# The last stage of a linear-attention and soft-MoE kernel: second layer and outputs by 256, 128 and 128 columns in place of 256 and 256, and a new order of steps on TensorE

## The chip, the cores and the metric

The kernel runs on one core of a Trainium2 chip. The metric is the device time of one execution in microseconds (us), lower is better. The runs of the kernel before took 341.94, 344.8 and 346.77 us, so the median is 344.8 us. One more execution was profiled; all rows of the trace are from that one.

A core has TensorE (PE: matmuls, with the weight loads listed as PEld), VectorE (DVE), ScalarE (ACT), GpSimd (POOL) and SyncE (SP), whose queue issues all DMAs of this kernel.

## The reference

Eight batches of eight heads of 576 tokens go through a linear attention with exponential features, and its output, 4608 tokens of 512 columns, through a soft mixture of eight experts with four slots each:

```python
q_p, k_p = phi(q), phi(k)                      # exp(+-(x w_phi - max|.|)), 256 features
kv  = einsum('bhsf,bhsd->bhfd', k_p, v)
x   = (q_p @ kv) / (q_p @ sum_s k_p + 1e-6)    # 4608 x 512 once the heads are side by side

logits = x @ phi                               # 4608 x 32 (8 experts x 4 slots)
d = softmax of logits over the 4608 tokens
slot_input = d.T @ x                           # 32 x 512
for e in range(8):
    h = maximum(slot_input[e] @ w1[e], 0)      # w1[e]: 512 x 1024
    slot_out[e] = h @ w2[e]                    # w2[e]: 1024 x 512
c = softmax of logits over the 32 slots
out = c @ slot_out                             # 4608 x 512
```

Only the last two products, `h @ w2[e]` and `c @ slot_out`, are touched by the change. All expert slots must be known before a single token can be written, so the whole output, 9.44 MB, leaves the core at the end.

## The kernel before

**Up to the last stage.** A list of tasks (`Plan`, with `ORDER` as the order written out by hand) runs the attention, the logits and the dispatch sums for the first 284 us or so. Weights are loaded in between, each of the 64 weight tiles (128 x 1024, 512 KB) with one DMA on SP's queue (L235): 32 tiles of `w1`, then 16 tiles of `w2` for output columns 0 to 255, then 16 tiles for columns 256 to 511. The later tiles reuse space that the attention gives back, and so are loaded late.

**The last stage** begins at L963. TensorE's instructions are issued there in exactly the order in which the program writes them (`manual_schedule(engines={PE})`); instructions of the other engines are put in order by the framework's scheduler, and start when their data is there. SP's queue issues the output DMAs one after the other.

- `layer1` (L841) makes `hp`, `hidden` (L894, L895) applies the maximum and the scale, and `picked` (L903, L906) turns the result and puts it into `sh`, with zeros in the places of other experts' slots.
- `layer2(a, e, cs)` (L932, L935) is the second layer of one expert for the 256 columns of half `a`. It is a sum over eight chunks `c` of 128 hidden units. A matmul has 32 weight columns (the slots) and 256 moving columns (of `w2`); four chunks run side by side in four column groups of the array. Every matmul stands in the trace as two instructions, so an expert and a half take 16 rows.
- `slots(a)` (L941, DVE) copies the sum out of PSUM. `slots2(a, ys)` (L948, L951) adds the four groups with a matmul by `rep` into `psy`, and an ACT copy and a DVE operation after it split the result into a rounded value and its rest: `yr`.
- `repeated(i)` (L617, POOL) and `combine(i)` (L921, L925, L926) prepare `cT[i]`, the combine weights of token group `i` (512 tokens, nine groups): four transposes on TensorE into `psc`, a rounding copy on ACT, and a subtraction on DVE that puts the rest in the lower half. Groups 0 to 2 are prepared earlier (L626, L630, L636); groups 3 to 8 in this stage.
- `output(a, i, yr)` (L959, L960, L961) makes 256 columns of 512 tokens: two matmuls with 512 moving columns into two of four PSUM banks, one copy by DVE and one by ACT into a tile `o`, and one 512 KB DMA. The matmul reads `yr` and `cT[i]`. The copies have to free a bank before the second next output can use it.

The order is a string: `C` is `combine` of the next group, `L` half an expert of `layer2` for columns 256 to 511, `o` the next output of columns 0 to 255, `r` is `slots2` of the first half, `s` and `R` are `slots` and `slots2` of the second. The nine outputs of the second half follow behind the string:

```python
TAIL = "CCLLrLLoLLCoLLCoLLCoLLCoLLoLoLsoRo"
```

Of the kernel before, what the change touches and what calls it, by code (L numbers as in the profile page):

```python
# [9 lines left out]
F32 = mybir.dt.float32  # L10
F32R = mybir.dt.float32r
AF = mybir.ActivationFunctionType
ALU = mybir.AluOpType
# [16 lines left out]
DM, NE, SPE, FF = 512, 8, 4, 1024  # L30
NS = NE * SPE
KC = DM // 128
FC = FF // 128
SP, PE, ACT, DVE, POOL = (getattr(mybir.EngineType, n) for n in ("SP", "PE", "Activation", "DVE", "Pool"))
NTT = B * S // 128
DH = DM // 2
# [7 lines left out]
NCT = 3  # L44
# [73 lines left out]

TAIL = "CCLLrLLoLLCoLLCoLLCoLLCoLLoLoLsoRo"


@with_exitstack
def tile_kernel(ctx: ExitStack, tc, xT, vv, w, phi, w1, w2, cst, out):
# [7 lines left out]
    nc = tc.nc  # L134
# [46 lines left out]
    for i in range(NWARM):  # L181
        ps = pmm.tile([128, 512], F32, tag="mm", name="psw")
# [9 lines left out]
    cs = const.tile([128, 257], F32, name="cs")  # L192
    ident = cs[:, 0:128]
    rep = cs[:, 128:256]
    low4 = cs[:, 256:257]
# [23 lines left out]
    keep = [10, 11, 12, 13]  # L219
    order = [j for j in range(nslot[-1]) if j not in keep]  # L220
    wt = []
    wpools = [wpool]

    def slot(j, name, dt=F32):
        return wpools[sum(j >= n for n in nslot)].tile([128, 1024], dt, tag=f"w{j}", name=name)
# [387 lines left out]
    cT = []  # L613
# [41 lines left out]
    for b in range(NB + 2):  # L655
# [10 lines left out]
        for p, (b_, u, t0, t1) in enumerate(pieces):  # L666
            if b_ == b:
                new, end = t0 == 0 or p == 0 or pieces[p - 1][0] != b, 4 * b + 4 == NT * u + t1
                n = t1 - t0
# [6 lines left out]
        q, bank = b - 2, [f"qb{b % 2}"]  # L676
# [6 lines left out]
    for s in range(NK):  # L683
        u, c = divmod(s, NCH)
        bp, h = divmod(u, H)
        n = bp, c
# [6 lines left out]
        if end:  # L693
            d = pick("kvcopy") == "d"
            p = max(i for i in range(len(pieces)) if pieces[i][1] == u)
# [21 lines left out]
        n = last_of[c] if final else 2 * bp + c // 2  # L717
# [119 lines left out]
    def layer1(a, kcs):  # L837
        for kc in kcs:
            for n in range(2):
                for e in range(4):  # L840
                    nc.tensor.matmul(hp[a][32 * e:32 * e + 32, n], si[:, kc],  # L841
                                     wt[(a * KC + kc) * 4 + e][:, n * 512:(n + 1) * 512],
                                     start=kc == 0, stop=kc == KC - 1, skip_group_check=True)
# [26 lines left out]
    def bank(shape, name):  # L870
        cps.append(cps.pop(0))
        return cps[-1][0].tile(shape, F32, tag=cps[-1][1], name=name)

    def lastw():
        for c in range(NCH):
            n = last_of[c]
            ps = bank([128, G, NS], "psL")
            turned(lTs.pop(n), ps)
            l = sm.tile([128, G, NS], F32, tag="eT", name="ls", bufs=3)
            nc.vector.tensor_copy(l, ps)  # L880
            wmax(n, l)
            wsub(n, nc.vector)
            wexp(n)
            wsum(n)
            wdiv(n, nc.vector)

    sh = []
# [4 lines left out]
    def hidden(a):  # L892
        t = slot(keep[a], "hs")
        nc.scalar.activation(t[:, 0:512], hp[a][:, 0], AF.Relu, scale=rs)  # L894
        nc.vector.tensor_scalar(t[:, 512:1024], hp[a][:, 1], rs, 0.0, op0=ALU.mult, op1=ALU.max)  # L895
        return t

    def picked(a, t):
        for i in range(2):
            ps = bank([128, FC // 2, 4, NS], "psh")  # L900
            for c in range(FC // 2):
                o = (FC // 2 * i + c) * 128
                nc.tensor.transpose(ps[:, c].rearrange("p e s -> p (e s)"), t[:, o:o + 128], ident)  # L903
            for e in range(4):
                c0 = (4 * a + e) * SPE
                nc.vector.tensor_copy(sh[a][:, e, FC // 2 * i:FC // 2 * (i + 1), c0:c0 + SPE], ps[:, :, e, c0:c0 + SPE])  # L906


    spare = [order[i] for i in range(len(wsrc) - nslot[-1], len(order)) if order[i] < NE * KC]
    gone = [i if i < nslot[-1] else order[i - nslot[-1]] for i in range(NE * KC, NE * (KC + 2))]  # L910
    cws, cts = [], []

    def repeated(i):
        if i % 2:
            cws.append(slot(spare[6 + i // 2 - 1], "cw").rearrange("p (g m) -> p g m", g=2))
        four(cws[-1][:, 1 - i % 2].rearrange("p (j m) -> p j m", m=128), i)

    def combine(i):
        ps = pd.tile([128, 4, 128], F32, tag="c", name="psc")
        for j in range(4):  # L920
            nc.tensor.transpose(ps[:, j], cws[(i - NCT) // 2][:, 1 - i % 2, j * 128:(j + 1) * 128], ident)  # L921
        if i % 2:
            cts.append(slot(spare[i // 2 - 1], "cT", F32R).rearrange("p (g m) -> p g m", g=2))
        x, ps = cts[-1][:, 1 - i % 2], ps.rearrange("p j m -> p (j m)")
        nc.scalar.copy(x, ps)  # L925
        nc.vector.tensor_tensor(x[64:128], ps[64:128], x[64:128].bitcast(F32), op=ALU.subtract)  # L926
        cT.append(x)


    yp = ph[0].tile([128, 2, 512], F32, tag="h", name="yp")  # L930

    def layer2(a, e, cs=range(FC)):  # L932
        for c in cs:
            g = 32 * (c % 4)
            nc.tensor.matmul(yp[g:g + 32, a, 0:DH], sh[e // 4][:, e % 4, c],  # L935
                             wt[NE * KC + (a * NE + e) * 2 + c // 4][:, (c % 4) * DH:(c % 4 + 1) * DH],
                             start=(e == 0 and c < 4), stop=(e == NE - 1 and c >= 4), skip_group_check=True)

    def slots(a):
        ys = slot(spare[3 + a], "ys")[:, 0:DH]  # L940
        nc.vector.tensor_copy(ys, yp[:, a, 0:DH])  # L941
        return ys

    yrs = slot(spare[5], "yr", F32R)

    def slots2(a, ys):
        ps = pd.tile([128, DH], F32, tag="c", name="psy")
        nc.tensor.matmul(ps, rep, ys, start=True, stop=True)  # L948
        yr = yrs[:, DH * a:DH * a + DH]

        yis = [nc.scalar.copy(yr, ps), nc.vector.scalar_tensor_tensor(yr, yr.bitcast(F32), low4, ps, op0=ALU.mult, op1=ALU.add)]  # L951
        return yr, yis[0].ins, yis[-1].ins

    def output(a, i, yr):

        o = slot(gone[i] if a == 0 else (gone[9:16] + keep[0:2])[i], "o").rearrange("p (b t) -> p b t", b=2)
        for b in range(2):
            ps = bank([128, 512], "pso")
            nc.tensor.matmul(ps, yr[:, b * 128:(b + 1) * 128], cT[i], start=True, stop=True)  # L959
            (nc.scalar.copy if b else nc.vector.tensor_copy)(o[:, b], ps)  # L960
        nc.sync.dma_start(out[a, i], o.rearrange("p b t -> p (b t)"))  # L961

    NO = NTT // 4  # L963
    with tc.manual_schedule(engines={PE}):
        layer1(1, range(0, 1))
        lastw()
        layer1(1, range(1, 2))
        picked(0, hidden(0))
        layer1(1, range(2, KC))
        layer2(0, 0)  # L970
        layer2(0, 1)
        picked(1, hidden(1))
        stacks["h"].close()
        pd = ctx.enter_context(tc.tile_pool(name="pd", bufs=2, space=PSUM, reuse_waits="tile"))
        for i in range(NCT, NO):
            repeated(i)
        for e in range(2, NE):
            layer2(0, e)
        ys = slots(0)
        cs, outs, l2 = iter(range(NCT, NO)), iter(range(NO)), iter(range(2 * NE))  # L980
        behind = ExitStack()
        for step in TAIL:
            if step == "L":
                e, i = divmod(next(l2), 2)
                layer2(1, e, range(4 * i, 4 * i + 4))
            elif step == "C":
                combine(next(cs))
            elif step == "o":
                output(0, next(outs), yr)
            elif step == "s":  # L990
                ys = slots(1)
            elif step == "r":
                yr, *_ = slots2(0, ys)
            else:
                yr2, *ins = slots2(1, ys)
                for x in ins:
                    behind.enter_context(tc.issue_after(x))
        behind.close()
        for i in range(NO):
            output(1, i, yr2)  # L1000


# [34 lines left out]
```

## Time and profile before

| what | value |
|---|---|
| runs | 341.94, 344.8, 346.77 us; median 344.8 |
| profiled execution | 344.9 us, of which the span of the trace 343.1 us |
| mean granted TensorE clock in the span | 0.984 of full speed |
| output DMAs | 18 of 512 KB, first issued at 313.73 us |
| median time of an output DMA from issue to landing | 3.7 us |

Rows of the timeline read: start in us, duration in us, engine, line, operation, tile written <- tiles read, shape, count of merged instructions, and in brackets the idle time of the engine ahead of it with what ended it. Rows of the chain of waits have start, duration, engine, tile and line; the chain is followed back from the last instruction. Rows of windows have, for a stretch of the span, the busy time (and number of instructions) of each engine, the granted TensorE clock as a share of full speed, the busy share of the DMA engines and the GB/s that they moved. In the views of DMA the GB/s are given in 40 equal slices of the stretch asked for. Matmuls overlap, so the durations of rows of single matmuls add up to more than the time that passes.

### The profile page before, as it was taken

Reading aid. Unit: us, or ns where it says so; the run is one execution under the profiler, and the core shown is the slowest. Engines: PE = TensorE matmul, PEld = TensorE weight load, DVE = VectorE, ACT = ScalarE, POOL = GpSimd, SP = SyncE. Lnnn points to the kernel's source line nnn. Section 1 sums busy time; section 2 is a strip of 40 time slices with the busy share of each in tenths; the row PEclk is TensorE's granted clock in tenths of the full one; section 3 lists DMA queues with packets and bytes.
Section 4 is the critical chain, followed back from the end, with each engine's and each line's share of the span. In section 5 each row is a group of like instructions: output and inputs, shape, how many; then the busy total and the mean of one; then the engine's idle time right before and its main releaser. Section 6 shows DMA issues by size and latency. Waiting matters only on the chain.

```text
span 343.1 us, 16153 instructions
## 1 busy us (share of the span) xinstructions
PE 327.2 (95%) x6825; PEld 271.1 (79%) x6825; DVE 243.6 (71%) x683; ACT 233.2 (68%) x677; POOL 168.0 (49%) x353
## 2 busy tenths in 40 slices
PE   8997999999999999999999999999999999999970
PEld 4896899998979999998899998979998753355430
DVE  1576487987787888887888888688886562615780
ACT  3897489968867888777789978677886250204470
POOL 1546466872356867561758758256664511130000
PEclk9999899999999999999999999999999999999995
DMA  6377256267234654674262844495426979998698
GB/s 223 117 238 257 83 196 226 67 208 285 66 111 155 204 166 165 210 302 118 58 195 61 320 154 149 162 319 176 128 76 233 352 297 406 408 406 333 282 400 324
DMA packets 22649, 74.09 MB, mean 216 GB/s; under 512 B 2992, under 2 KB 3248, under 8 KB 22576
## 3 DMA queue, kind: packets, MB, share of 16 engines
q1 hardware_dynamic: 22576, 73.05, 60.1%
q8 instruction: 54, 0.88, 1.0%
q14 instruction: 19, 0.16, 0.1%
HBM read 63.60 MB, written 9.44 MB: 213 GB/s over the span
## 4 chain that ended last, share of the span: by engine, by line
PE 92%; DVE 2%; ACT 2%; issue 1%; POOL 1%; ACTq 0%; POOLq 0%
PE kvp L311 23%; PE psn L364 20%; PE psq L264 12%; PE psk L264 10%; PE psx L734 5%; PE yp L935 4%; PE hp L841 4%; PE pso L959 3%; PE psl L417 2%; PE pss L456 2%; PE psw L183 1%; PE psc L921 1%; PE psd L449 1%; PE pss L559 1%; PE psh L903 1%
## 5 line engine op out<-in xcount | busy, mean ns | idle before, releaser
L284 POOL TENSOR_TENSOR vs<-vt,mk 128x520 f32<-128x520 f32 (+3 forms) x128 | 91.6, 730 | 63.3 <-ACT mk L273 42.6
L311 PE MATMUL kvp<-vs,kf 128*64 128x65 f32 (+1 forms) x2304 | 93.3, 230 | 1.9 <-issue 1.9
L311 PEld LDWEIGHTS kvp<-vs,kf 128*64 128x64 f32 x2304 | 81.8, 138 | 9.3 <-issue 5.4
L364 PE MATMUL psn<-kvs,qf 128*64 128x65 f32 x2304 | 82.1, 222 | 0.8 <-issue 0.8
L264 PE MATMUL psq<-xs,wd 64*128 64x128 f32 x576 | 78.7, 284 | 0.0
L264 PE MATMUL psk<-wd,xs 64*128 64x128 f32 x576 | 77.4, 283 | 0.6 <-ACT kf L298 0.4
L364 PEld LDWEIGHTS psn<-kvs,qf 128*64 128x64 f32 x2304 | 74.5, 138 | 3.4 <-issue 1.4
L264 PEld LDWEIGHTS psq<-xs,wd 64*128 64x128 f32 x576 | 69.2, 190 | 3.7 <-issue 1.1
L264 PEld LDWEIGHTS psk<-wd,xs 64*128 64x128 f32 x576 | 68.4, 190 | 4.1 <-ACT kf L298 1.3
L269 DVE TENSOR_REDUCE mk<-psk 128x4 f32<-128x512 f32 x72 | 48.4, 678 | 17.2 <-PE psk L264 8.0
L331 ACT ACTIVATE qf<-psq 128x512 f32<-128x512 f32 x72 | 42.7, 595 | 20.0 <-DVE mts L326 5.9
L326 DVE TRANSPOSE_TENSOR_REDUCE mts<-psq 128x16 f32<-128x512 f32 x72 | 50.7, 706 | 7.6 <-PE psk L264 3.6
L295 ACT ACTIVATE kf<-psk 128x512 f32<-128x512 f32 x72 | 42.6, 592 | 18.7 <-DVE mk L269 7.6
L406 POOL TENSOR_TENSOR xc<-un,dn 128x256 f32<-128x256 f32 x64 | 39.2, 614 | 12.6 <-PE pss L456 6.6
L375 DVE TENSOR_TENSOR un<-psn,eq 128x195 f32<-128x195 f32 x96 | 33.1, 348 | 16.3 <-PE psn L364 12.6
L334 ACT ACTIVATE qf<-psq 128x512 f32<-128x512 f32 x72 | 42.9, 601 | 0.4 <-DVE mts L326 0.2
L298 ACT ACTIVATE kf<-psk 128x512 f32<-128x512 f32 x72 | 42.6, 596 | 0.0
L342 ACT ACTIVATE mh<-mts 32x36 f32<-32x36 f32 x128 | 29.4, 230 | 7.5 <-DVE mts L326 5.9
L380 DVE TENSOR_TENSOR un<-psn,un 128x195 f32<-128x195 f32 x96 | 33.2, 349 | 1.1
L348 DVE TENSOR_REDUCE eq<-mh 32x9 f32<-32x36 f32 x128 | 26.4, 206 | 2.6 <-ACT mh L342 1.1
L272 ACT ACTIVATE mk<-mk 128x4 f32<-128x4 f32 x72 | 15.1, 210 | 4.0 <-DVE mk L269 3.4
L351 POOL TENSOR_TENSOR eq<-eq 128x9 f32<-128x9 f32 x32 | 6.5, 203 | 22.0 <-DVE eq L348 22.0
(130 smaller groups left out, 342.4 us busy)
## 6 DMA issues: line engine op xcount, KB each, us to landing
wt<-w SPq DMA_DIRECT2D x64, 512.0 KB, 7.0
xs<-xT SPq DMA_DIRECT2D x36, 512.0 KB, 4.2
vt<-vv SPq DMA_DIRECT2D x32, 325.0 KB, 3.3
out<-o SPq DMA_DIRECT2D x18, 512.0 KB, 3.7
xs<-xT SPq DMA_DIRECT2D x2, 128.0 KB, 2.5
cs<-cst SPq DMA_DIRECT2D x1, 128.5 KB, 4.0
wd<-w SPq DMA_DIRECT2D x1, 64.0 KB, 2.1
phs<-phi SPq DMA_DIRECT2D x1, 64.0 KB, 3.8
```

The lines of the kernel that those rows point to most:

```text
L264: nc.tensor.matmul(ps, l, r, start=True, stop=True)
L269: nc.vector.tensor_reduce(km[b][:, 2], kx[b], axis=AX, op=ALU.max, apply_absolute_value=True)
L284: nc.gpsimd.tensor_tensor(vs[b][:, :, place(b, u, t, o):place(b, u, t, o) + n], v[:, t + o:t + o + n].unsqueeze(1).broadcast_to([128, 2, n ...
L295: nc.scalar.activation(kf[b][:, 1], kx[b], AF.Exp, scale=-1.0)
L298: nc.scalar.activation(kf[b][:, 0], kx[b], AF.Exp)
L311: nc.tensor.matmul(ps[f:f + FE // 2, pn, o:o + m], kf[b][:, pn, NT * u + t - 4 * b, f:f + FE // 2], v2[:, pn, at:at + m], start=(t == 0 an ...
L326: nc.vector.tensor_reduce(mts.rearrange("p r j -> p j r")[:, o:o + 4], qx[b].rearrange("p j (r t) -> p (j r) t", t=32), axis=AX, op=ALU.ma ...
L331: nc.scalar.activation(qf[b][:, 0], qx[b], AF.Exp)
L334: nc.scalar.activation(qf[b][:, 1], qx[b], AF.Exp, scale=-1.0)
L364: nc.tensor.matmul(ps[64 * f:64 * f + 64, j, pn], q2[:, pn, 64 * f:64 * f + 64], kv[:, pn, b2], start=True, stop=True)
L380: nc.vector.tensor_tensor(x, nx.pop(s)[:, :, 1], x, op=ALU.add)
L406: nc.gpsimd.tensor_tensor(x[:, :, h * D:(h + 1) * D], un[u][:, a:b, 0:64], dn[u][:, a:b].unsqueeze(2).broadcast_to([128, b - a, 64]), op=A ...
```

## The change

The columns of the second layer and of the output are cut in three parts `q`: 0 to 255, 256 to 383 and 384 to 511 (`COLS`). `layer2(q, e)` now does a whole expert (all eight chunks) for one part; its matmuls have 256 moving columns for part 0 and 128 for parts 1 and 2, and parts 0 and 2 use the same PSUM bank. `slots`, `slots2` and `output` take the part instead of the half. An output of part 0 is still two matmuls, two copies and a 512 KB DMA (its copies for groups 3 and 7 both go to ACT). An output of parts 1 and 2 is one matmul and one copy (DVE and ACT in turn), and each second one issues a 512 KB DMA with the columns of both; the ninth group of either part issues one of 256 KB. The output in memory has another layout, with the same bytes, and 19 DMAs.

The order is new. `L` is a whole expert of part 1 and then of part 2, `s` and `r` serve every part, and `o` takes the next output from a list that each `r` lengthens by nine:

```diff
-TAIL = "CCLLrLLoLLCoLLCoLLCoLLCoLLoLoLsoRo"
+COLS = (0, 256), (256, 128), (384, 128)
+TAIL = "sCroooo" "CoCoLLLCoCoLLLCoLLsr" "LLoooLLooLLooLLsroo" "ooooooooo"
+def quarter(q, i):
+    return (i, q) if q < 2 else (17, q - 2) if i == 8 else (1 + 4 * q + i // 2, i % 2)
...
-    def layer2(a, e, cs=range(FC)):
-        for c in cs:
-            g = 32 * (c % 4)
-            nc.tensor.matmul(yp[g:g + 32, a, 0:DH], sh[e // 4][:, e % 4, c],
-                             wt[NE * KC + (a * NE + e) * 2 + c // 4][:, (c % 4) * DH:(c % 4 + 1) * DH],
+    def layer2(q, e):
+        c0, w = COLS[q]
+        for c in range(FC):
+            g, o = 32 * (c % 4), c % 4 * DH + c0 % DH
+            nc.tensor.matmul(yp[g:g + 32, q % 2, 0:w], sh[e // 4][:, e % 4, c],
+                             wt[NE * KC + (c0 // DH * NE + e) * 2 + c // 4][:, o:o + w],
...
-    def output(a, i, yr):
-        o = slot(gone[i] if a == 0 else (gone[9:16] + keep[0:2])[i], "o").rearrange("p (b t) -> p b t", b=2)
-        for b in range(2):
+    def output(q, i, yr):
+        for b in range(COLS[q][1] // 128):
+            n, k = quarter(COLS[q][0] // 128 + b, i)
+            if n not in os:
+                os[n] = slot((gone + keep[0:2])[n], "o").rearrange("p (b t) -> p b t", b=2)
             ps = bank([128, 512], "pso")
-            nc.tensor.matmul(ps, yr[:, b * 128:(b + 1) * 128], cT[i], start=True, stop=True)
-            (nc.scalar.copy if b else nc.vector.tensor_copy)(o[:, b], ps)
-        nc.sync.dma_start(out[a, i], o.rearrange("p b t -> p (b t)"))
+            nc.tensor.matmul(ps, yr[:, 128 * b:128 * b + 128], cT[i], start=True, stop=True)
+            (nc.scalar.copy if (k + (n == 17)) % 2 or (q == 0 and i % 4 == 3) else nc.vector.tensor_copy)(os[n][:, k], ps)
+        if k or n == 17:
+            o = slice(0, 2) if n < 17 else slice(k, k + 1)
+            nc.sync.dma_start(out[n, :, o], os[n][:, o])
...
-        ys = slots(0)
-        cs, outs, l2 = iter(range(NCT, NO)), iter(range(NO)), iter(range(2 * NE))
+        cs, l2 = iter(range(NCT, NTT // 4)), iter((q, e) for q in (1, 2) for e in range(NE))
+        ys, outs = [], []
         for step in TAIL:
             if step == "L":
-                e, i = divmod(next(l2), 2)
-                layer2(1, e, range(4 * i, 4 * i + 4))
+                layer2(*next(l2))
             elif step == "C":
                 combine(next(cs))
             elif step == "o":
-                output(0, next(outs), yr)
+                output(*outs.pop(0))
             elif step == "s":
-                ys = slots(1)
-            elif step == "r":
-                yr, *_ = slots2(0, ys)
+                ys.append(slots(len(ys)))
             else:
-                yr2, *ins = slots2(1, ys)
-                for x in ins:
-                    behind.enter_context(tc.issue_after(x))
+                q = len(ys) - 1
+                yr, ins = slots2(q, ys[q])
+                outs += [(q, i, yr) for i in range(NTT // 4)]
+                if q == 2:
+                    for x in ins:
+                        behind.enter_context(tc.issue_after(x))
         behind.close()
-        for i in range(NO):
-            output(1, i, yr2)
```

More of the change, by code (lines that the diff above doesn't have):

```diff
@@ L937, in layer2, with slots, slots2 @@
                              start=(e == 0 and c < 4), stop=(e == NE - 1 and c >= 4), skip_group_check=True)
-    def slots(a):
-        ys = slot(spare[3 + a], "ys")[:, 0:DH]
-        nc.vector.tensor_copy(ys, yp[:, a, 0:DH])
+    def slots(q):
+        ys = slot(spare[3 + q % 2], "ys")[:, 0:COLS[q][1]]
+        nc.vector.tensor_copy(ys, yp[:, q % 2, 0:COLS[q][1]])
         return ys
     yrs = slot(spare[5], "yr", F32R)
-    def slots2(a, ys):
-        ps = pd.tile([128, DH], F32, tag="c", name="psy")
+    def slots2(q, ys):
+        c0, w = COLS[q]
+        ps = pd.tile([128, w], F32, tag="c", name="psy")
@@ L948, in slots2 @@
         nc.tensor.matmul(ps, rep, ys, start=True, stop=True)
-        yr = yrs[:, DH * a:DH * a + DH]
-        yis = [nc.scalar.copy(yr, ps), nc.vector.scalar_tensor_tensor(yr, yr.bitcast(F32), low4, ps, op0=ALU.mult, op1=ALU.add)]
-        return yr, yis[0].ins, yis[-1].ins
-    def output(a, i, yr):
-        o = slot(gone[i] if a == 0 else (gone[9:16] + keep[0:2])[i], "o").rearrange("p (b t) -> p b t", b=2)
-        for b in range(2):
-            ps = bank([128, 512], "pso")
-            nc.tensor.matmul(ps, yr[:, b * 128:(b + 1) * 128], cT[i], start=True, stop=True)
-            (nc.scalar.copy if b else nc.vector.tensor_copy)(o[:, b], ps)
-        nc.sync.dma_start(out[a, i], o.rearrange("p b t -> p (b t)"))
@@ L963, in tile_kernel @@
-    NO = NTT // 4
+        yr = yrs[:, c0:c0 + w]
+        return yr, [nc.scalar.copy(yr, ps).ins,
+                    nc.vector.scalar_tensor_tensor(yr, yr.bitcast(F32), low4, ps, op0=ALU.mult, op1=ALU.add).ins]
+    os = {}
+    def output(q, i, yr):
[3 more added lines that the diff above has]
+                os[n] = slot((gone + keep[0:2])[n], "o").rearrange("p (b t) -> p b t", b=2)
+            ps = bank([128, 512], "pso")
+            nc.tensor.matmul(ps, yr[:, 128 * b:128 * b + 128], cT[i], start=True, stop=True)
[3 more added lines that the diff above has]
+            nc.sync.dma_start(out[n, :, o], os[n][:, o])
@@ L974, in tile_kernel @@
         pd = ctx.enter_context(tc.tile_pool(name="pd", bufs=2, space=PSUM, reuse_waits="tile"))
-        for i in range(NCT, NO):
+        for i in range(NCT, NTT // 4):
             repeated(i)
@@ L1029 @@
     aps = [nc.dram_tensor(n, a.shape, mybir.dt.from_np(a.dtype), kind="ExternalInput").ap() for n, a in arrays.items()]
-    o = nc.dram_tensor("out", (2, NTT // 4, 128, 2 * 512), F32, kind="ExternalOutput").ap()
+    o = nc.dram_tensor("out", (18, 128, 2, 512), F32, kind="ExternalOutput").ap()
     with tile.TileContext(nc) as tc:
@@ L1033 @@
     r = run_bass_kernel_spmd(nc, [arrays], core_ids=[0])
-    y = np.asarray(r.results[0]["out"]).reshape(2, NTT // 4, 128, 2, 512).transpose(1, 4, 0, 3, 2).reshape(NTT // 4, 512, DM)
+    y = np.asarray(r.results[0]["out"]).reshape(18, 128, 2, 512)
+    y = np.stack([np.concatenate([y[n, :, k].T for n, k in (quarter(q, i) for q in range(4))], axis=1) for i in range(NTT // 4)])
     return np.concatenate([np.concatenate([y[2 * b], y[2 * NBP, 128 * b:128 * b + 128], y[2 * b + 1]]) for b in range(NBP)])
```

## The prediction

> **What bounds the kernel now.** I read the page first, then the windows of the last 30 us, then the chain of waits there, and last the timeline row by row around the first output. Only the part behind 308.6 us changes, so all else keeps its time. The windows tell which resource sets the pace:
>
> ```profile
> span 343.1 us, 16153 instructions
> HBM read 63.60 MB, written 9.44 MB: 213 GB/s over the span
> 305.00:310.00 5.00, 5.00 (x86) 3.09 (x80) 0.51 (x2) 0.70 (x2) 0.00 (x0) 1.00 1.03 407
> 310.00:315.00 5.00, 5.00 (x58) 2.25 (x47) 2.46 (x5) 1.63 (x4) 0.00 (x0) 1.00 0.86 338
> 315.00:320.00 5.00, 5.00 (x61) 2.63 (x60) 3.64 (x6) 2.93 (x6) 0.00 (x0) 1.00 0.69 283
> 320.00:325.00 5.00, 5.00 (x51) 2.31 (x44) 3.40 (x6) 2.25 (x4) 0.00 (x0) 1.00 0.64 258
> 330.00:335.00 5.00, 2.84 (x10) 1.25 (x8) 3.34 (x6) 3.15 (x6) 0.00 (x0) 1.00 1.02 404
> 335.00:340.00 5.00, 0.00 (x0) 0.00 (x0) 0.00 (x0) 0.00 (x0) 0.00 (x0) 0.54 1.02 407
> GB/s 437 364 437 455 419 382 346 437 382 419 382 400 419 382 401 382 437 419 400 419 401 437 401 382 437 382 437 401 382 455 382 419 401 382 455 382 382 346 164 91
> GB/s 414 388 414 423 414 405 362 336 397 414 397 371 405 423 414 397 405 414 414 414 388 414 405 414 405 414 405 397 379 414 397 405 414 414 207 0 0 0 0 0
> ```
>
> The reader is to see three stretches. Until 313.6 us the DMA engines are full with weights (the first GB/s row is 305 to 314 us in slices of 0.225 us; it falls in the last two). From 315 to 325 us they move only 283 and 258 GB/s, since TensorE is the bound. From 325 us on they are full again, and they alone set the end: the second GB/s row is 325 to 344 us in slices of 0.475 us, so the last byte goes at 341.4 us and the span ends 1.7 us later. At about 405 GB/s the 9.44 MB need 23.3 us. From 313.6 us that would be 336.9; it was 341.4, so the DMA engines idled 4.5 us. This is all that an earlier supply of outputs can win.
>
> The middle stretch in the chain of waits and the timeline:
>
> ```profile
> 316.13 0.59 PE psc L921 x4
> 316.72 0.47 PE pso L959 x2
> 317.19 1.00 PE yp L935 x16
> 318.19 0.59 PE psc L921 x4
> 326.98 5.87 PE pso L959 x18
> 82.87 1.01 PE psl L417 x32
> ```
> ```profile
> 308.61 1.09 PE L921 MATMUL psc<-cs,cw 128*128 128x128 f32 x8
> 308.75 0.42 DVE L941 COPY ys<-yp 128x256 f32<-128x256 f32 x1 [4.93 <-PE yp L935]
> 309.30 1.07 ACT L925 CAST cT<-psc 128x512 fp32r<-128x512 f32 x2 [7.86 <-PE psc L921]
> 309.92 1.30 DVE L926 TENSOR_TENSOR cT<-psc,cT 64x512 fp32r<-64x512 f32 x2 [0.75 <-ACT cT L925]
> 310.67 0.30 PEld L948 LDWEIGHTS psy<-ys,cs 128*128 128x128 f32 x2 [0.45 <-DVE cT L926]
> 311.41 0.37 ACT L951 CAST yr<-psy 128x256 fp32r<-128x256 f32 x1 [1.03 <-PE psy L948]
> 311.81 0.48 DVE L951 SCALAR_TENSOR_TENSOR yr<-yr,cs,psy 128x256 fp32r<-128x256 f32 x1 [0.59 <-ACT yr L951]
> 312.34 0.30 PEld L959 LDWEIGHTS pso<-xT,yr 128*128 128x128 f32 x2 [0.46 <-DVE yr L951]
> 312.88 0.69 DVE L960 COPY o<-pso 128x512 f32<-128x512 f32 x1 [0.59 <-PE pso L959]
> 313.12 0.59 ACT L960 COPY o<-pso 128x512 f32<-128x512 f32 x1 [1.34 <-PE pso L959]
> 313.73 24.29 SPq L961 DMA_DIRECT2D out<-o  x18
> 316.06 0.42 PEld L921 LDWEIGHTS psc<-cs,cw 128*128 128x128 f32 x4 [0.41 <-issue]
> 316.76 0.58 ACT L925 CAST cT<-psc 128x512 fp32r<-128x512 f32 x1 [0.98 <-PE psc L921]
> 317.71 0.69 DVE L926 TENSOR_TENSOR cT<-psc,cT 64x512 fp32r<-64x512 f32 x1
> 295.30 0.28 DVE L880 COPY ls<-psL 128x128 f32<-128x128 f32 x1
> GB/s 426 393 404 350 186 66 109 404 360 426 164 22 262 415 415 306 0 87 404 404 415 88 0 306 382 437 273 44 109 371 404 393 77 350 437 415 372 437 404 382
> ```
>
> One output with one `C` and one expert-half pair takes TensorE 0.59 + 0.47 + 1.00 = 2.06 us, against 1.29 us that its 512 KB need at 405 GB/s. No row of this loop waits for a `cT`: the string keeps two `C` ahead of the first `o`, so each `cT` is at least one round old when its output needs it. What a `cT` costs is in the rows all the same: 0.70 us from the transposes' first load to the ACT copy (316.06 to 316.76), 0.62 to the DVE subtraction (309.30 to 309.92), 0.69 for it, and 0.05 back to TensorE (as `yr`: 311.81 + 0.48 to 312.34). That is 2.06 us from `C` to a matmul that reads it.
>
> **The change part by part.** The instructions themselves are nearly free. A matmul of 32 weight columns and 128 moving ones is in the trace already: 32 rows of L417 in 1.01 us, 31.6 ns each. An expert of part 1 or 2 is 16 such rows, 0.51 us; 16 experts are 8.1 us, where 128 rows at 62.5 ns (16 in 1.00) were 8.0. The nearest bounds are half the 256-column row, 31.3 ns, and the whole of it, 62.5; I take the row with the very shape, and 0.15 us for each switch into `L` (1.00 for 16 is 0.12 more than a pure rate of 55 ns would make). Output matmuls, copies and bytes are the same; one DMA more and one more `s` and `r` round come in. The two 256 KB DMAs could at worst cost a whole 512 KB time each, 1.3 us together; I take nothing, as the bytes are the same.
>
> The order is what counts. Group 3 is prepared ahead of `oooo`, and then comes `CoCo`: group 4's `C` stands directly ahead of output 4, which reads that very `cT`. TensorE runs in the written order, so it waits out the 2.06 us, and queued behind the waiting matmul are the next `C` (so nothing overlaps), the `LLL` behind it, and with them all of parts 1 and 2; SP's queue waits too. A `Co` costs 2.06 + 0.47 = 2.53 us, and `L` is no cover, since it stands behind it.
>
> I follow TensorE on the clock of the trace of before. `C` at 308.61; `psy` behind its four transposes at 309.2; ACT writes `yr` 0.74 later (310.67 to 311.41); DVE is busy with group 3's subtraction until 309.92 + 0.69 = 310.6, then 0.48 for `yr`: first `o` at 311.14, which is 1.2 us earlier than before. Its DMA follows 1.39 us later (312.34 to 313.73), at 312.5, while the weights still fill the queue: the start is covered. The second follows by 0.47, the third and fourth by 0.65 (18 matmuls of 9 outputs in 5.87 us, bound by the copies): next `C` at about 313.6. ACT has by then five copies of 0.585 us from 311.92 on (group 3 has two) and is free at 314.85, so output 4 is at 314.85 + 0.62 + 0.69 + 0.05 = 316.2. `C` 316.7; its ACT copy waits for output 4's, until 317.57; output 5 at 318.93. `LLL`, 1.52 + 0.15: 321.1. `C`, output 6 at 323.16, `C`, output 7 at 325.9 (its ACT copy again behind output 6's), `LLL` to 328.05, output 8 at 330.1; `LL` to 331.75. `s` (0.28 for 128 columns) and `psy` to 332.55, `LL` to 333.7, where `yr` is just ready. First outputs of part 1 at 333.75 and 334.0; their common DMA is issued at 335.15, and its bytes flow 0.75 us later (before, 313.73 to the slice at 314.5 in the third GB/s row, which is 312 to 327 us by 0.375), at 335.9.
>
> By then the nine outputs of part 0 are long gone: the last is issued at 331.5. What is left is half of all bytes, 4.72 MB, 11.65 us. Part 1's pairs come every 1.65 us (`LL` 1.16, two outputs 0.47), 0.36 slower than the DMA, twice: 0.7 us. The third `s` and `r` hold up the fourth pair by about 1.0 us, for their copies on ACT stand behind `yr`. Behind that, part 2 has no `L` and makes a pair in 0.65 us, so the DMA is full. Last byte at 335.9 + 11.65 + 1.7 = 349.25, span 1.7 more: 350.95, or 7.85 us over 343.1. The profiled execution took 344.9, so 352.75 at full clock.
>
> The clock has to be added. The trace has one gap of TensorE in mid-kernel:
>
> ```profile
> 34.92 1.25 PE L311 MATMUL kvp<-vs,kf 128*64 128x65 f32 x10 [1.92 <-issue]
> 31.65:35.06 3.41, 1.49 (x49) 1.36 (x45) 1.91 (x6) 2.11 (x6) 1.53 (x4) 1.00 0.87 299
> 35.06:38.48 3.42, 3.42 (x32) 3.08 (x32) 0.28 (x1) 0.17 (x1) 1.22 (x2) 0.50 0.44 150
> 325.20:328.61 3.41, 2.90 (x11) 1.58 (x10) 2.88 (x6) 2.38 (x5) 0.00 (x0) 1.00 0.97 392
> ```
>
> Behind a stretch of 3.41 us with 1.49 us (44%) of work the clock was 0.50 for the next 3.41 us; behind one with 2.90 us (85%) it was not. In `CoCo` a stretch of that length, say 314.96 to 318.38, holds one output (about 0.5 us of tail) and one `C` (0.66): near 34%, under the row that tripped. Then half clock falls on `LLL` (1.15 us of it done in the 2.3 us left) and delays what follows by some 1.4 us. No delay, where the gate isn't tripped, is one end; the other is half clock from 318.4 to part 1, which doubles 1.5 + 1.5 + 1.0 us of `L` and three transposes and outputs, about 7. I take 1.4, one tripped stretch, by the row at 44%, and come to 354.2, say 354; against the median of 344.8, which the profiled 344.9 matches, that is 2.7% more.
>
> [...]
>
> **The rivals.**
> - The clock stays full although TensorE waits: 352.75, with 350 to 353.5 by the small terms. For it: the stretch at 34% has two short gaps, the one that tripped has a single one of 1.92 us. Against it: 34% is under 44%. Chance 0.24.
> - Half clock nearly all the way from 318 us to part 1, if the limit lies nearer 85% than 44%: +7, about 360. For it: no stretch between 44% and 85% is in the trace; stretches with `LLL` in them come to 55 to 80%. Chance 0.14.
> - Not slower: the queue of outputs hides the waits for `cT`, because four outputs are ready early and the first DMA starts under the weights. Then only the 4.5 us of idle DMA count: 344.9 - 4.5 = 340.4, and with a round of `s` and `r` uncovered up to 344. It decides at 1.29 us for an output: were `Co` no longer than that, DMA would never run dry. For it: ACT needs 1.17 and DVE 1.38 us a round. Against it: the dependence is in the same round, 2.53 us. Chance 0.1.
>
> **How the numbers follow.** My forecast, waits for `cT` and about one stretch at half clock, 352.5 to 357, has 0.46; with the three rivals that is 0.94, and 0.06 lies elsewhere. The range of 349 to 361 leaves out the rival that isn't slower, and some of the long half clock and the rest. Two per cent, about what a measurement of this kernel can tell from no change, is 6.9 us: slower means over 351.7. The forecast, the long half clock and over half of the full-clock case lie above: 0.74. The rest of the full-clock case and nearly all of the other side lie within: 0.24. Faster by over 2% would be under 337.9, below the 340.4 that full DMA engines allow: 0.02.
>
> **What would show it.** Right: TensorE's matmuls of L921's successor followed by about 2 us until the next output, with the DVE subtraction named as the releaser; output DMAs 4 to 8 some 2.5 us apart or more, holes in the GB/s between 319 and 336 us, the first DMA of part 1 at about 335, full GB/s behind it, a stretch with clock 0.50. Wrong: outputs every 1.3 us up to the ninth, GB/s full from 313 us on, and an end before 344; or a layer of 128 columns that takes over 0.6 us an expert, which would put the loss elsewhere.

## The result, and the profile after

The changed kernel took 351.79, 356.53, 356.7 and 358.03 us, median 356.62; the kernel before, on the same chips, 341.22 to 346.77, median 343.37. The ratio is 1.034, with a 95% interval of 1.027 to 1.041. Ratios here and below are formed from fast runs alone (358.03 us is a slow one), medians from all runs, so a ratio is not the quotient of two medians. The forecast was 354 us, 349 to 361, slower.

The profiled execution took 356.7 us with a span of 354.9 us. Parts that are the same in both kernels differ by some us from one execution to the next: the first `C` (transposes of group 3, right behind part 0's layer) starts at 306.62 us here and at 308.61 us before. So below I also count the **tail**, from the first load of that `C` to the end of the span: 343.1 - 308.61 = 34.5 us before, 354.9 - 306.62 = 48.3 us after.

The windows of the changed kernel, in the columns of those shown of before (PE, PEld, DVE, ACT, POOL busy; clock; DMA share; GB/s):

```profile
310.00:315.00 5.00, 3.09 (x14) 1.89 (x13) 2.79 (x5) 3.24 (x7) 0.00 (x0) 0.97 1.02 410
315.00:320.00 5.00, 3.60 (x42) 2.38 (x44) 1.70 (x3) 1.62 (x3) 0.00 (x0) 0.50 0.75 303
320.00:325.00 5.00, 3.04 (x30) 1.99 (x22) 1.39 (x2) 1.54 (x3) 0.00 (x0) 0.84 0.20 84
325.00:330.00 5.00, 4.10 (x51) 2.91 (x52) 0.69 (x1) 1.19 (x3) 0.00 (x0) 0.50 0.51 210
330.00:335.00 5.00, 3.60 (x38) 2.37 (x37) 1.39 (x2) 1.17 (x2) 0.00 (x0) 0.50 0.02 7
335.00:340.00 5.00, 4.58 (x87) 2.92 (x83) 2.04 (x5) 1.20 (x3) 0.00 (x0) 0.98 0.38 152
```

Three columns tell the story together. The DMA engines are full up to 315 us (before, up to 313.6) and then move 84 GB/s from 320 to 325 us and 7 from 330 to 335, where before they moved 258 and 404. TensorE is not full in the same stretches, and neither are DVE and ACT: nobody is the bound by its busy time, so somebody waits for a chain. And the clock column, which stood at 1.00 before up to 335 us, shows 0.50 in three of these rows and 0.84 in one.

The chain of waits names the chain, and the view of waits its sum (us in total, times, longest):

```profile
314.08 0.74 PE pso L972 x2
314.82 0.85 PE psc L928 x4
315.67 0.02 issue
315.70 0.59 ACT cT L932
316.29 0.02 issue
316.31 0.70 DVE cT L933
317.02 0.04 issue
317.06 1.22 PE pso L972 x2
318.29 2.72 PE yp L943 x48
...
336.26 1.01 PE yp L943 x32
```
```profile
PEld pso L972 <- DVE cT L933: 9.0, 5, 2.1
```

One round reads: an output's matmuls, then the transposes of the next group, the ACT copy and the DVE subtraction one after the other, and only then the next output's matmuls, 2.98 us behind the start of the last ones (314.08 to 317.06). Five such waits make 9.0 us. The three experts behind them (`yp`, 48 rows: one whole expert is 16 rows, eight matmuls of two instructions each) take 2.72 us, 56.7 ns a row, in a stretch at half clock; at full clock the 32 rows at 336.26 take 31.6 ns each. The first outputs of part 1 are reached at 337.2 us, as this piece of the timeline shows, where the kernel before had its whole layer done by 324.8:

```profile
335.77 0.30 PEld L957 LDWEIGHTS psy<-ys,cs 128*128 128x128 f32 x2 [0.85 <-DVE ys L949]
337.20 0.53 PEld L972 LDWEIGHTS pso<-xT,yr 128*128 128x128 f32 x3 [0.20 <-DVE yr L961]
```

### The profile page after: what moved, and what is told of

It reads as the page before. It is cut to its first block, busy times and chain, and to the rows that moved or that the text cites. A ratio compares the mean times of both kernels' runs of the same rounds, so it can differ in the third digit from the quotient of the medians.

```text
span 354.9 us, 16416 instructions
## 1 busy us (share of the span) xinstructions
PE 332.4 (94%) x6954; PEld 277.5 (78%) x6955; DVE 242.7 (68%) x683; ACT 234.2 (66%) x680; POOL 168.1 (47%) x353
## 4 chain that ended last, share of the span: by engine, by line
PE 86%; DVE 4%; DMA 3%; ACT 2%; issue 2%; POOL 1%; ACTq 0%; POOLq 0%; DVEq 0%
PE kvp L318 22%; PE psn L371 20%; PE psq L271 11%; PE psk L271 9%; PE psx L741 4%; PE hp L848 4%; PE yp L943 3%; DMA wt<-w 3%; PE pso L972 3%; PE psl L424 2%; PE pss L463 2%; PE psw L190 1%; DVE cT L933 1%; DVE o L973 1%; ACT cT L932 1%
## 5 line engine op out<-in xcount | busy, mean ns | idle before, releaser
L271 PE MATMUL psq<-xs,wd 64*128 64x128 f32 x576 | 77.6, 281 | 0.0
L271 PE MATMUL psk<-wd,xs 64*128 64x128 f32 x576 | 76.3, 281 | 0.7 <-ACT kf L305 0.4
L271 PEld LDWEIGHTS psq<-xs,wd 64*128 64x128 f32 x576 | 68.0, 188 | 3.7 <-issue 1.1
L271 PEld LDWEIGHTS psk<-wd,xs 64*128 64x128 f32 x576 | 67.3, 188 | 4.1 <-ACT kf L305 1.4
L973 ACT COPY o<-pso 128x512 f32<-128x512 f32 x20 | 11.1, 588 | 14.6 <-PE pso L972 14.6
L943 PE MATMUL yp<-wt,sh 128*32 128x128 f32 (+1 forms) x384 | 19.1, 359 | 0.0
```

The lines of the kernel that those rows point to most:

```text
L271: nc.tensor.matmul(ps, l, r, start=True, stop=True)
```

## The experiments

Seven kernels were run, all but `filled2`, which has a single run, several times against the kernel before on the same chip. Each ratio goes with the median of before in its own row. Tails are from one profiled execution of each kernel.

| kernel | columns | order of `C` | median us | before, median us | ratio to before (95%) | tail, us |
|---|---|---|---|---|---|---|
| before | 256, 256 | early | 343.37 | | 1 | 34.5 |
| changed | 256, 128, 128 | late | 356.62 | 343.37 | 1.034 (1.027 to 1.041) | 48.3 |
| `c_ahead` | 256, 128, 128 | early | 344.79 | 345.07 | 0.9985 (0.995 to 1.002) | 34.9 |
| `halves_late_c` | 256, 256 | late | 355.28 | 345.07 | 1.026 (1.018 to 1.034) | 46.4 |
| `cols_old_order` | 256, 128, 128 | early, order of before | 345.8 | 345.07 | 1.002 (0.998 to 1.006) | 35.7 |
| `filled` | 256, 128, 128 | late, waits filled | 351.0 | 345.07 | 1.020 (1.013 to 1.027) | 42.0 |
| `filled2` | 256, 128, 128 | late, less filled | 352.73, one run | 344.07 | none | 42.0 |
| `early_o` | 256, 128, 128 | early, own order | 342.25 | 344.07 | 0.996 (0.9935 to 0.9988) | 33.3 |
| `covered` | 256, 128, 128 | early, own order | 342.48 | 344.07 | 0.995 (0.992 to 0.9985) | 32.8 |

The theory on trial is the prediction's: TensorE waits for a `cT` that is written in the same round, and half clock behind the waits adds to it. The main rival is that the columns cost: narrow matmuls, one more round of `s` and `r`, smaller DMAs.

**`c_ahead`: every `C` earlier, all else in its order**

```diff
-"sCroooo" "CoCoLLLCoCoLLLCoLLsr"
+"sCCroCoCoCoCoo" "LLLooLLLoLLsr"
```

> Only the places of C in the order differ from the changed kernel: every cT is prepared at least three outputs ahead; outputs and layer keep their order. Theory (the loss is TensorE waiting for a cT written in the same round): the five waits of about 2 us go, 9.0 us of idle before L972 by the DVE subtraction fall under 1; no stretch at half clock before the last outputs. The two transposes groups ahead of r delay the first output by 0.6 us; eight outputs by about 322 us, first DMA of part 1 at about 328 in place of 335-339, then 11.65 us of DMA and the known small gaps: span about 343 to 345, ratio to the kernel before 0.99 to 1.01. Rival (narrow parts, the extra s and r round or the smaller DMAs cost it): the waits go, but the ratio stays above 1.02, span 350 or more.

The ratio is 0.9985: the whole loss is gone. In the chain of waits of this kernel the three experts come earlier and at full clock, and the last `psy` too:

```profile
316.37 1.45 PE yp L943 x48
...
329.64 0.50 PE psy L957 x2
```

Of the outputs' weight loads only one still waits for a `cT`, 0.2 us:

```profile
PEld pso L972 <- DVE cT L933: 0.2, 1, 0.2
```

The clock is 1.00 until the last output. What came late in its place is small: two `C` ahead of `r` take both of the PSUM buffers that they share with `psy`, and `psy` waits 1.2 us for the first subtraction. The columns and the number of experts, outputs and DMAs are those of the changed kernel, so none of these made the loss. The span, 341.7 us, came out below the 343 to 345 expected, in an execution that reached the tail 1.8 us before the one of the kernel before.

**`halves_late_c`: the old columns with the late `C`**

```diff
-TAIL = "CCLLrLLoLLCoLLCoLLCoLLCoLLoLoLsoRo"
+TAIL = "CrooooCoCoLLLLLLCoCoLLLLLLCoLLLLsR"
```

> The kernel before with its 256 and 256 columns, and only its string of steps changed: group 4 to 8 are prepared directly ahead of their own output, as in the changed kernel, LLL becoming LLLLLL half experts. Theory (order alone): output 8 issued at about 331.5 us of the old clock, second yr at 334.6, 11.65 us of DMA behind 336.8: span 350 at full clock, up to 355 with stretches at half clock, ratio 1.02 to 1.035. Rival (the columns are what costs): ratio below 1.01.

The string alone makes the kernel before slower, by 2.6% with an interval from 1.8 to 3.4%. The waits are the same five:

```profile
PEld pso L959 <- DVE cT L926: 8.4, 5, 1.7
```
```profile
319.35 5.09 PE yp L935 x48
...
329.78 2.73 PE yp L935 x48
```

The second view is the chain of waits. The same 48 rows take 5.09 us where all but the last 0.3 us are at half clock (up to 324.12), and 2.73 at full clock.

**`cols_old_order`: the new columns with the early `C`**

```diff
+TAIL = "sCCLLrLLoLLCoLLsCorLLCoLLCoLLoLoLsoro" "ooooooooo" "ooooooooo"
```

> The changed kernel's columns of 256, 128 and 128, with the order of the kernel before: two C ahead of the first output, a pair of L per output, the s and r of part 1 put in where its eight experts are done. Theory (the columns are neutral): TensorE's chain as before plus 0.5 us of psy, 128-column experts at 0.5 us: span 342 to 344.5, ratio 0.99 to 1.01. Rival (narrow columns cost): experts over 0.6 us, ratio above 1.02.

The ratio is 1.002 with 1 inside the interval. With `c_ahead` this closes the square of columns and order: early `C` gives 1.00 with either columns, late `C` 1.026 and 1.034. The columns by themselves neither win nor lose what can be measured here.

**`filled` and `filled2`: the waits stay, TensorE is kept busy in them**

`x` is a view of the constants as bf16; `f` stands between each late `C` and its output, and behind the first `r`.

```diff
+        cs_ = cs[:, 0:256]
...
+            elif step == "f":
+                x = cs_.bitcast(mybir.dt.bfloat16)
+                for _ in range(5):
+                    nc.tensor.matmul(yp[:, 0], x[:, 0:128], x, start=True, stop=True, skip_group_check=True)
...
+"sCrfoooo" "CfoCfoLLLCfoCfoLLLCfoLLsr" ...
```

> The changed kernel with five matmuls of 128x512 bf16 (about 0.21 us each at full clock) put on TensorE between each C and the output that waits for it, and between r and the first output; they write a PSUM bank that nobody reads then. The waits for cT stay as long, but TensorE is busy in them. Theory (waits halve the clock, and the clock is a part of the loss by itself): granted clock 1.00 from 310 us to the last outputs, LLL back from 2.7 to about 1.6 us, span 349 to 350.5, ratio to before 1.015 to 1.025. Rival A (the halving has nothing to do with waiting): clock at 0.50 in the same share, span 354 to 356. Rival B (the fillers get in the way): outputs later than 2.6 us a round, span above 355.

> As the run with five filling matmuls in each wait, with two. In the runs so far the clock was halved behind stretches of 3.41 us in which TensorE was busy 1.84 us or less, and stayed full behind 1.96 us or more. Theory (the busy share of a stretch decides): two fillers lift the stretches with waits from 1.3-1.6 us to about 2.0-2.3, so the clock stays 1.00 and the span is 347.5 to 350, as with five. Rival (the length of a single idle gap decides): gaps of about 1 us remain in each round; the clock would be halved again in some stretches, span over 351.

The views of `filled` (chain of waits, then waits):

```profile
316.73 1.45 PE yp L943 x48
318.17 0.60 PE psc L928 x4
318.77 0.02 issue
318.80 0.59 ACT cT L932
319.42 0.70 DVE cT L933
320.12 0.04 issue
320.16 0.74 PE pso L972 x2
```
```profile
PEld pso L972 <- DVE cT L933: 4.6, 5, 1.2
```

The round from `C` to its output is as in theory, 1.99 us (318.17 to 320.16), with the five fillers in it for 1.24 us (from 318.60), and the DMA engines starve as in the changed kernel (146 to 162 GB/s from 320.3 to 334 us). What is gone is half clock: the experts take 1.45 us for 48 rows. The tail falls from 48.3 to 42.0 us, the median from 356.6 to 351.0. So 6.3 us of the profiled tail, 5.6 us of the median, were the clock, and 42.0 - 34.9 = 7.1 us the waits themselves. The split is that of one execution of each kernel: the profiled one of the changed kernel has the lowest mean clock of its four, and the intervals of the two ratios to the kernel before meet at 1.027. Within that, work that nobody needs made the kernel faster.

With two fillers in place of five the clock stays at 1.00 too, and the tail is 42.0 us again (308.87 to 350.9). The total of 352.73 us is a single run that reached the tail 2.95 us later than `filled` did; the span of 350.9 lies just outside of the 347.5 to 350 expected for that reason. The rival (span over 351 with halved stretches) is refuted by the clock, which was full, rather than by the span.

**`early_o` and `covered`: an order that feeds the DMA engines**

The string of `early_o`, and below it that of `covered`, which differs in the first three pieces:

```diff
-TAIL = "sCroooo" "CoCoLLLCoCoLLLCoLLsr" "LLoooLLooLLooLLsroo" "ooooooooo"
+TAIL = "sCrCoCoCoCoCo" "LLLoLLoLLLsoro" "ooLLooLLooLLLLsooro" "ooooooooo"
```
```diff
+TAIL = "sCrLCoCoCoCoCo" "LLoLLoLLLsorLo" "ooLLooLLooLLLsooro" "ooooooooo"
```

> The changed kernel's columns with another order: group 3 ahead of r as in the changed kernel, every later C ahead of the output before its own, five outputs at once, then the eight experts of part 1 in pieces of two and three between outputs, s and r of part 1 ahead of the last two outputs of part 0, and the outputs of part 1 in pairs ahead of each pair of experts. Theory (the DMA engines idle only where the next part's yr comes late): first output at about 309.3 us, DMA full from the weights on; the gap between part 0 and part 1 under 1 us in place of about 3, a gap of 1 to 2 us ahead of part 2; span 339.5 to 341.5, ratio to the kernel before 0.985 to 0.995. Rival (TensorE's own work up to the last r bounds it, whatever the order): last r as late as with the C ahead alone, 329.6 us, ratio 0.998 or more.

> As the run before, and one expert is put behind each of the first two r, where TensorE would wait for yr. Theory: TensorE has work in both waits, so the last r comes 0.5 to 1 us earlier than in the run before; span 338.5 to 341, ratio 0.98 to 0.993, against a floor of about 338 where the DMA engines never idle. Rival: these waits were not on the path (the copies on DVE and ACT are), ratio as in the run before within 0.003.

Both are a little faster than the kernel before, by 0.4 and 0.5%, with intervals that end just below 1. Both gained less than their theories said, and under 1% by either interval. (In the string of `early_o`, as in that of the kernel before, every `C` from group 4 on has four outputs between itself and its own, not one.) The first outputs of part 2 in the timelines of `c_ahead`, `early_o` and `covered`:

```profile
330.87 0.97 PE L972 MATMUL pso<-xT,yr 128*128 128x512 f32 x3 [0.27 <-DVE yr L961]
331.23 0.96 PE L972 MATMUL pso<-xT,yr 128*128 128x512 f32 x3 [0.76 <-DVE yr L961]
333.96 0.96 PE L972 MATMUL pso<-xT,yr 128*128 128x512 f32 x3 [0.75 <-DVE yr L961]
```

They come 24.0, 23.5 and 22.5 us behind the first `C` of each (306.85, 307.7 and 311.45). `early_o` lies between its theory and its rival: the order moved this point, which hangs on TensorE's own work up to the last `r`, by half a microsecond only. In `covered` it comes a microsecond earlier still, as was expected, but the ratio is within 0.003 of that of `early_o`, as its rival said. So whether the two experts moved into the waits are worth anything in the total can't be told from these runs.

## Why the prediction was right, and where it was off

**The wait.** The step that carried the forecast held: TensorE issues in the written order, `C` stands directly ahead of the output that reads its `cT`, and a round then costs 2.06 + 0.47 us. At full clock the way from `C` to its output measured 1.99 us in `filled`. `c_ahead` and `halves_late_c` show both directions: the late `C` taken away, and put in alone.

**The sum at full clock.** The prediction's tail without the clock ended at 350.95 us, 42.3 us behind its first `C` at 308.61. The two kernels with the clock kept full measured 42.0. The steps on the way agree as well: behind the first `C` the prediction has output 8 at 21.5 us and the first output of part 1 at 25.1, and `filled` has 21.0 (326.96) and 24.6 (330.54). One sign did not come: full GB/s behind the first DMA of part 1. The changed kernel moved 152 and 264 GB/s from 335 to 345 us; the sum had 1.7 us for such gaps, the list of signs had none. The timed run at 351.79 us, with a span of 350.0 and a mean clock of 0.994, and the 351.0 of `filled` stand beside the 352.75 worked out.

**The cost of the columns at nothing.** Held: 31.6 ns a row was taken from L417 and is what the 32 rows at 336.26 us show, 1.01 us.

**The clock.** Half clock came behind the waits, as expected, but the size was wrong: the term of one half-clock stretch, 1.4 us, measured 6.3 us in the profiled tail. That the total of 356.7 us lies only 2.5 us over the 354.2 of the sum is in part luck: this execution reached its first `C` 2.0 us earlier than the one that the sum started from; counted by the tail, 48.3 us stand against 42.3 + 1.4 = 43.7. The execution had two stretches at half clock from 314.72 and three from 324.96, with one at full clock between. A stretch is 3.41 us long here: the changes of the clock at 314.72, 321.55, 324.96 and 335.20 us lie 6.83, 3.41 and 10.24 us apart, that is two, one and three times 3.41 us. The error was to expect half clock only behind stretches about as empty as the one row at 44%, and to reckon only those of plain `CoCo` among them. Rows of stretches of this length, counted from a change of the clock in each trace, block by block of the changed kernel, `halves_late_c`, `cols_old_order` and `filled2`, show busy time and clock in this stage (first column of numbers behind the length: PE busy; third from the end: the clock in that stretch):

```profile
311.31:314.72 3.41, 1.57 (x9) 1.06 (x9) 1.20 (x3) 1.99 (x4) 0.00 (x0) 1.00 1.03 411
314.72:318.13 3.41, 2.01 (x7) 1.04 (x5) 1.52 (x3) 1.17 (x2) 0.00 (x0) 0.50 0.99 400
318.13:321.55 3.42, 3.42 (x52) 2.75 (x52) 0.46 (x1) 0.58 (x1) 0.00 (x0) 0.50 0.50 202
321.55:324.96 3.41, 1.49 (x9) 0.87 (x7) 1.39 (x2) 1.50 (x3) 0.00 (x0) 1.00 0.00 0
324.96:328.37 3.41, 2.47 (x30) 1.73 (x34) 0.69 (x1) 1.23 (x3) 0.00 (x0) 0.50 0.38 154
328.37:331.79 3.42, 2.52 (x32) 1.67 (x24) 0.25 (x1) 0.58 (x1) 0.00 (x0) 0.50 0.37 153
331.79:335.20 3.41, 2.91 (x34) 1.89 (x34) 1.14 (x2) 0.58 (x1) 0.00 (x0) 0.50 0.08 31
335.20:338.61 3.41, 2.99 (x61) 2.10 (x61) 1.51 (x4) 0.85 (x2) 0.00 (x0) 1.00 0.32 130
```
```profile
313.88:317.29 3.41, 1.34 (x8) 0.79 (x6) 1.62 (x3) 1.86 (x4) 0.00 (x0) 1.00 1.03 411
317.29:320.70 3.41, 2.57 (x18) 1.24 (x22) 1.39 (x2) 0.65 (x2) 0.00 (x0) 0.50 0.84 335
320.70:324.12 3.42, 3.42 (x40) 1.45 (x32) 0.00 (x0) 0.00 (x0) 0.00 (x0) 0.50 0.41 165
327.53:330.94 3.41, 1.96 (x27) 1.10 (x30) 1.51 (x3) 1.33 (x3) 0.00 (x0) 1.00 0.37 154
330.94:334.36 3.42, 2.16 (x36) 1.07 (x25) 0.61 (x1) 0.59 (x1) 0.00 (x0) 1.00 0.37 153
```
```profile
330.45:333.87 3.42, 1.84 (x6) 0.94 (x6) 2.57 (x4) 2.07 (x4) 0.00 (x0) 1.00 1.02 408
333.87:337.28 3.41, 0.00 (x0) 0.00 (x0) 0.00 (x0) 0.00 (x0) 0.00 (x0) 0.50 1.02 401
```
```profile
314.32:317.73 3.41, 2.00 (x12) 1.06 (x10) 1.39 (x2) 1.86 (x5) 0.00 (x0) 1.00 1.01 408
317.73:321.14 3.41, 2.39 (x52) 1.61 (x52) 1.39 (x2) 1.04 (x2) 0.00 (x0) 1.00 0.82 323
```

Each row is read with the next one: the busy time of a stretch, and the clock of the one that follows. At full clock, 1.34, 1.49, 1.57 and 1.84 us of 3.41 were followed by 0.50; 1.96 and 2.00 were followed by 1.00. So in these rows 54% is the highest share that was followed by half clock, and 57% the lowest that was followed by full. At half clock 2.01, 2.47, 2.52 and 2.57 were followed by half clock again, 2.91 and 3.42 by full. These rows at half clock are what the prediction lacked: the stretches from 314.72, 324.96 and 328.37 us had 2.01, 2.47 and 2.52 us of busy time, more than the 1.96 that left the clock full, and half clock followed all the same, though the work in them takes longer (48 rows of `yp` 2.72 us against 1.45 in `filled`).

Rows of earlier stages don't all fit these figures. The first two are consecutive stretches of `halves_late_c`, in the attention; the third is of the kernel before:

```profile
33.98:37.39 3.41, 1.77 (x29) 1.53 (x29) 1.08 (x4) 0.82 (x4) 1.04 (x3) 1.00 0.91 311
37.39:40.80 3.41, 3.41 (x100) 3.29 (x98) 2.87 (x8) 2.88 (x10) 1.55 (x4) 1.00 0.05 17
24.83:28.24 3.41, 2.60 (x64) 2.27 (x59) 2.98 (x8) 3.19 (x10) 2.68 (x7) 1.00 0.58 187
```

There 1.77 us was followed by full clock, less than the 1.84 us that was followed by half; the matmuls are others there (`kvp`, `psk` and `psq`). So the busy time of a stretch alone doesn't tell the clock behind it, and the expectation of `filled2` states its two figures too generally. The third row has 2.60 us, 76%, and the clock stayed full behind it: the prediction's "no stretch between 44% and 85%" overlooked it, and with it the two rows to choose between would have been those at 44 and 76%.

Which stretches are at half clock in other executions is not shown, for only one execution of a kernel has a trace: the four runs of the changed kernel have mean clocks of 0.967, 0.976, 0.977 and 0.994 at spans of 354.9, 354.7, 356.2 and 350.0 us.

**The rivals.** Half clock nearly all the way, at 0.14, was nearest to the profiled execution; the clock that stays full, at 0.24, fits one timed run of four by its time (351.79 us) and its mean clock (0.994). That the queue would hide the waits fell on the point named for it: a round of 2.5 us against 1.29 us of DMA.

## What to carry to other kernels

Where one engine's order is written by hand, count for every step how far ahead its input is started: here a chain through two other engines cost its whole length where the reader stood right behind it (1.99 us from `C` to its output in `filled`), and 0.2 us of waits for a `cT` in all where steps enough lay in between (`c_ahead`; three outputs or more in the early orders, and how few would do was not tried). When the bound is a queue of transfers, an order that brings the first ones early wins nothing if the supply behind them is slower than the transfers: here the first output DMA came at 310.58 us in place of 313.73, and the kernel lost. And the waits on TensorE cost more than their length here: the tail of the changed kernel is 13.4 us longer than that of `c_ahead` (48.3 against 34.9), of which 7.1 us were the waits and 6.3 us half clock. Look at the clock column first, as useless work in the wait may cost less than an idle wait (351.0 against 356.62 us here).

## What the runs showed of the hardware

- In the changed kernel's trace the granted clock went between 1.00 and 0.50 at 314.72, 321.55, 324.96 and 335.20 us, which are 6.83, 3.41 and 10.24 us apart. In the rows of this stage shown above, by stretches of 3.41 us, full clock was followed by half behind 1.34, 1.49, 1.57 and 1.84 us of busy time and by full behind 1.96 and 2.00; half clock was followed by half behind 2.01, 2.47, 2.52 and 2.57 us and by full behind 2.91 and 3.42. In the attention 1.77 us left it full, so busy time alone doesn't tell it; what does, stays open.
- The longest idle time of TensorE ahead of an output in the changed kernel was 1.84 us (ahead of 314.08), and the clock was halved at 314.72. In `filled2`, with two matmuls of 128x512 in each wait whose result nobody reads (0.45 us for the two at 314.50 in its chain of waits), it stayed at 1.00 through this stage up to the last outputs.
- In the layer of the changed kernel, matmuls of 32 weight columns and 128 moving ones (two rows of the trace each) took 31.6 ns a row at full clock (32 rows in 1.01 us) and 56.7 ns at half clock (48 rows in 2.72 us).
